# Attention with top-32 masking and a channel mix: twelve transposes of the identity for each of the first 20 tiles, and a new order

## Chip, cores and metric

The kernel runs on one core of a Trainium2 chip. The metric is the time of one execution on the device in microseconds; the median of several runs is compared. The engines are TensorE (PE), VectorE (DVE), ScalarE (ACT), GpSimd (POOL) and SyncE (SP, which here issues most DMAs). PEld is TensorE's loading of the stationary operand.

## The reference

For each of 8 batches and 8 heads, attention over 576 rows with head size 64, in which a row keeps only its 32 largest scores. The heads are joined to rows of 512, and a channel mix follows.

```python
scores = scale * np.matmul(q, k.transpose(0, 1, 3, 2))
kth = np.partition(scores, -top_k, axis=-1)[..., -top_k:-top_k + 1]      # top_k = 32
scores = np.where(scores >= kth, scores, -1000000000.0)
attn = np.exp(scores - np.max(scores, axis=-1, keepdims=True))
attn = attn / (np.sum(attn, axis=-1, keepdims=True) + 1e-09)
x = np.matmul(attn, v)                    # then (B, S, H * D)
...
xk = mu_k * x + (1.0 - mu_k) * x_prev     # x_prev: the row before
xr = mu_r * x + (1.0 - mu_r) * x_prev
k = np.maximum(xk @ w_k, 0.0)             # 512 to 1024
v = k * k @ w_v                           # 1024 to 512
r = 1.0 / (1.0 + np.exp(-(xr @ w_r)))
return r * v
```

## The kernel before

The attention is cut into 288 tiles of 128 rows by 576 columns, in 64 visits (batch, half of the rows, pair of heads). For one tile, TensorE computes the scores (`score` and `sliver`, L836 to L845, for two tiles at once), ScalarE copies them out of PSUM (`keep`, L850), VectorE finds the top values in seven pieces and then over all pieces (`cand`, `best`, `drop`, L855 to L860), GpSimd and ScalarE prepare the exact 32nd value (`under`, `count`, `below`, L866 to L871), VectorE picks it (`eighth`, `nine`, L872 and L874), ScalarE takes the exponential (`exps`, L877), and VectorE masks (`mask`, L880). TensorE then turns the masked tile in four transposes (`turn`, L885) plus one for the last 64 columns of two tiles (`turnl`, L894), ScalarE copies the result out (`et`, `el`), TensorE multiplies with v (`weigh`, L907 and L908), and VectorE scales the sum and puts it into `xT`, the input of the mix (`place`, L940 and L943).

The mix works on 18 chunks of 256 rows. GpSimd and ScalarE form the mixed input and split it in a high and a low part (`change`, `share`, `add`, `xh`, `xl`, L1009 to L1023), in two halves of the channels. TensorE multiplies each product three times, for the parts (L629 to L631): `hidden`, `gate` and `value`. The weights of the mix are unpacked at the start from pieces that DMAs bring (`weight`, L1085 to L1119), 20 blocks: eight of w_k, four of w_r (blocks 8 to 11), eight of w_v (blocks 12 to 19). In each, ScalarE, VectorE (`wshift` L1107, `wexp` L1112 or L1115, `wrest` L1117) and GpSimd (`wput` L1110 or L1114, `wmul` L1119) take part.

Three PSUM buffers called `rot` serve in turn the transposes, the mix's results and two steps of each weight block (`wabs` writes one that `wshift` reads, `wrest` one that `wfine` reads).

The order of work on each engine is written out ahead by a planner (`Plan.run`). Each step has a lane, a cost, its dependences and a key: the number of its tile plus an offset by name (`OFF`, with `FIRST`, `HEAD` and `TAIL` added at the beginning and the end). Among the steps of an engine that could start within `NEAR` of the earliest, the one with the lowest key goes first. Chunks are due by `AT` and `STEP`, the blocks of w_k, w_r and w_v by `WAT`, `LWAT`, `VWAT` and their steps, as in

```python
key = WAT + n * WSTEP if name == "k" else LWAT + n * LWSTEP if name == "r" else VWAT + n * VWSTEP
```

The engines then follow that order strictly; only the waits for data and buffers are left to the chip. The planner also has a model of TensorE's clock (`Clock`). One step called `warm` exists before: twelve transposes of the identity into a `rot` buffer at the very start (L1165), which nothing reads.

Of the kernel before, what the change touches and what calls it, by code (L numbers as in the profile page):

```python
# [37 lines left out]
OFF = dict(kt=-149.064, kq=-2.447, v=48.118, zero=104.971, score=-11.554, keep=-135.674, cand=6.552, best=-17.933, drop=-182.956, under=-102.12,  # L38
           count=-18.516, below=-102.498, eighth=9.321, nine=-50.972, exps=1.133, mask=-104.109, turn=-50.435, et=29.287, turnl=-30.586, el=-75.416,
           weigh=-30.634, inv=-20.812, inv2=-135.01, turni=-51.051, ri=36.948, place=-115.941, lowest=61.461, ranks=-134.855, mu=49.321, nmu=-39.508,  # L40
           changek=138.702, sharek=94.164, addk=371.12, xhk=24.993, xlk=-36.33, sharer=185.332, addr=48.759, xhr=89.136, xlr=-20.192, hidden=37.203,
           relu=-241.476, sq=56.91, r2=31.986, hl=54.569, gate=371.368, gexp=-213.982, value=170.367, gated=-58.13, store=-42.377, w=98.749,
           wabs=-68.48, wshift=-51.265, wsign=-219.747, wexp=100.695, wfine=-65.07, whi=-150.349, wmul=130.665, spread=-57.351, sliver=-131.257,
           low=-35.741, lowt=224.106, lowr=-284.336, lowc=45.392, wrest=-86.41, wm=235.872, wput=20.784, warm=99.586)
CANDS, BESTS = 0.117, -2.501
STEP, WAT, WSTEP, GATE, VALUE, PACE = 17.949, 2.161, 10.191, 3.223, 5.257, -2.0
# [20 lines left out]
BONUS = {("S", "W"): -33.418, ("T", "W"): 15.751, ("R", "W"): -30.909, ("T", "S"): 43.457, ("R", "S"): 49.885, ("W", "S"): -6.906, ("S", "R"): 36.783, ("T", "R"): 80.901, ("W", "R"): 94.651, ("R", "R"): 7.145, ("S", "S"): 77.39, ("R", "T"): 24.499, ("W", "W"): 40.464, ("Z", "S"): -129.751, ("W", "Z"): 71.854, ("S", "T"): -42.48, ("Z", "W"): -24.105, ("Z", "R"): 67.5, ("T", "Z"): 89.886, ("S", "Z"): -8.015, ("R", "Z"): 22.532, ("Z", "Z"): -71.918, ("Z", "T"): -14.968, ("W", "T"): 46.183, ("T", "T"): 3.444}  # L67
# [9 lines left out]
FIRST = dict(kt=9.824, kq=-62.943, v=-7.675, zero=98.267, score=-88.574, keep=25.077, cand=79.22, best=-29.451, drop=34.008, under=-44.481,  # L77
             count=-127.038, below=49.932, eighth=18.033, nine=10.948, exps=-14.36, mask=16.168, turn=-256.513, et=-60.13, turnl=-83.593, el=-13.794,
             weigh=-260.993, inv=-50.965, inv2=3.265, turni=-147.57, ri=147.35, place=-108.029, ranks=17.752, mu=-58.715, nmu=-156.45,
             changek=-29.419, sharek=-4.307, addk=-163.022, xhk=-50.628, xlk=-9.955, sharer=25.165, addr=164.205, xhr=170.896, xlr=133.774,  # L80
             hidden=96.642, relu=0.545, sq=-37.562, r2=115.817, hl=14.536, gate=-161.398, gexp=-55.717, value=-74.447, gated=159.726, store=210.93,
             w=56.679, wabs=-227.205, wshift=-93.047, wsign=-16.424, wexp=-30.394, wfine=-79.085, whi=-11.933, wmul=-42.277, spread=-24.769,
             sliver=51.45, wrest=39.226, wm=-303.52, wput=-24.756, low=83.408, lowr=-56.354, lowest=31.336, lowc=58.647, lowt=-61.014, warm=-7.404)
HEAD = dict(sharek=-70.074, zero=132.48, lowt=-39.544, store=225.857, el=-126.117, gate=-70.119, turni=111.107, sq=28.568, hl=61.165, relu=-14.297,
            wmul=-44.021, low=-21.718, xhk=28.236, inv=115.831, v=-51.162, gated=-129.248, xlk=-0.117, turn=40.157, r2=45.071, xlr=19.366,
            addr=-165.161, ri=-78.566, below=-8.543, best=-17.781, wabs=-86.745, lowr=134.423, sliver=-82.002, nmu=9.399, kq=160.097, changek=27.051,
            count=-9.443, hidden=66.556, addk=-87.675, xhr=104.686, lowc=84.506, eighth=-58.165, w=141.91, kt=-10.884, wshift=-13.321, wexp=-8.43,
            ranks=142.708, spread=48.261, mask=-39.589, whi=123.677, drop=-118.7, gexp=49.552, keep=-138.746, inv2=-12.512, mu=-108.325,
            weigh=-103.636, turnl=25.74, score=-76.981, under=-103.491, nine=-89.251, place=24.804, sharer=58.037, et=-8.177, wfine=-20.05,
            wsign=-173.139, exps=-57.171, lowest=-65.114, value=140.622, cand=-8.009, wrest=-4.191, wm=-7.658, wput=-29.71, warm=23.458)  # L90
TAIL = dict(addr=83.707, wshift=-99.353, wexp=96.445, sq=187.355, lowt=-151.412, sliver=-139.369, whi=-38.32, xlk=48.2, xhk=84.256, store=-74.037,
            nine=25.418, best=87.475, lowr=86.936, hl=97.628, turni=-78.124, xhr=72.803, relu=-35.414, kt=-29.128, drop=64.837, gate=-78.823,
            eighth=-59.927, under=25.811, inv2=-93.695, v=54.202, w=-106.308, wmul=-55.614, wfine=97.246, lowest=-122.151, gexp=120.926,
            score=-1.911, sharek=-46.119, wabs=-131.815, exps=22.349, nmu=-219.708, below=41.819, changek=-48.432, lowc=-8.068, inv=338.652,
            low=-35.808, gated=98.664, turnl=32.405, place=105.089, ri=117.337, r2=-73.571, weigh=-94.945, spread=-190.521, kq=-26.094, cand=63.03,
            value=42.206, hidden=-49.814, zero=106.116, ranks=-16.901, mu=134.337, count=48.088, mask=103.11, wsign=19.05, xlr=59.381, keep=-49.002,
            addk=60.223, el=-37.043, sharer=-138.117, turn=6.568, et=-21.007, wrest=62.833, wm=-176.605, wput=-87.431, warm=-32.933)
# [89 lines left out]
class Plan:  # L187
# [8 lines left out]
    def buf(self, name):  # L196
        return Buf(self.kinds[name])
# [226 lines left out]
def topk_attention_channel_mix(ctx: ExitStack, tc: tile.TileContext, q, k, v, mu_kr, w_k, w_v, w_r, out):  # L424
# [359 lines left out]
    def attend(plan, visits, X, pair_sums):  # L784
# [8 lines left out]
        for p, (b, hp, part) in enumerate(visits):  # L793
# [21 lines left out]
            for i in part:  # L815
# [48 lines left out]
                def sn(T, w):  # L864
# [415 lines left out]
```

## Time and profile before

| | |
|---|---|
| median of 3 runs | 1150.0 us (1149.75 to 1151.17) |
| profiled execution, its own time | 1152.01 us |
| its span, first to last instruction | 1150.2 us |
| mean granted TensorE clock | 0.978 |
| TensorE busy | 1088.8 us (95%) |
| VectorE busy | 1063.4 us (92%) |
| ScalarE busy | 1005.8 us (87%) |
| GpSimd busy | 930.0 us (81%) |

The shares are averages over a head, a long middle part and an end, which have to be read apart. The granted clock is a record of the throttle on TensorE: 1.00 is 2.4 GHz, and a stretch wholly at 1.2 GHz would show 0.50. In rows of instructions the first number is the start in microseconds from the beginning of the span, the second how long the merged group took, `x` how many instructions it holds; a bracket at the end gives the idle time of the engine before the group and what ended it.

### The profile page before, as it was taken

To read this page: it belongs to the slowest core of one execution; us is meant where nothing else is said; L and a number is where in the kernel's file an instruction comes from. 1 tells how busy PE (TensorE), PEld (TensorE's weight loads), DVE (VectorE), ACT (ScalarE), POOL (GpSimd) and SP (SyncE) were. 2 spreads that over 40 slices of the span, in tenths; PEclk is the share of its full clock that TensorE was granted. 3 is DMA by queue.
4 is the path that set the end of the run, shared out by engine and by line. 5 is a ranking of instruction groups with operands and counts; after the bars stand their busy time and mean duration, and the time that the engine had idled before them with its cause. 6 is when DMAs were issued, how large, how long until landed. Compare 5 with 4: busy or idle time off the path is not lost. (4 is left out here: it accounts for less than half of the span.)

```text
span 1150.2 us, 27623 instructions
## 1 busy us (share of the span) xinstructions
PE 1088.8 (95%) x8637; PEld 844.7 (73%) x8637; DVE 1063.4 (92%) x5741; ACT 1005.8 (87%) x2129; POOL 930.0 (81%) x1153
## 2 busy tenths in 40 slices
PE   6556789999999999999999999999999999999998
PEld 3343567778787777777777878787878787877886
DVE  7999999999999999999999999999999999999600
ACT  6878999999999999999999989999999989889641
POOL 4787898788887888878799888888797889788773
PEclk9777999999999999999999999999999999999999
DMA  8743332211221112111211112111221122110000
GB/s 281 265 133 105 126 105 79 70 55 34 77 72 42 53 60 84 57 65 56 76 59 43 58 58 79 50 56 65 67 68 34 44 82 78 51 39 22 20 19 22
DMA packets 38891, 83.64 MB, mean 73 GB/s; under 512 B 4432, under 2 KB 12624, under 8 KB 38736
## 3 DMA queue, kind: packets, MB, share of 16 engines
q1 hardware_dynamic: 38448, 81.41, 21.5%
q8 instruction: 70, 1.15, 0.4%
q14 instruction: 85, 0.70, 0.2%
q10 hardware_dynamic: 288, 0.39, 0.1%
HBM read 72.35 MB, written 9.44 MB: 71 GB/s over the span
## 5 line engine op out<-in xcount | busy, mean ns | idle before, releaser
L871 POOL TENSOR_TENSOR sg<-sc,sg 128x576 f32<-128x576 f32 x288 | 410.0, 1426 | 83.5 <-ACT sg L869 79.7
L855 DVE MAX8 cand<-sc 128x8 f32<-128x82 f32 (+1 forms) x2016 | 378.0, 230 | 4.8 <-ACT sc L850 3.8
L877 ACT ACTIVATE se<-sc,seen 128x576 f32<-128x576 f32 x288 | 216.4, 751 | 23.6 <-DVE E L880 21.7
L869 ACT ACTIVATE sg<-sc,seen 128x576 f32<-128x576 f32 x288 | 224.8, 781 | 12.8 <-POOL seen L866 11.6
L880 DVE SCALAR_TENSOR_TENSOR E<-sc,seen,se 128x576 f32<-128x576 f32 x288 | 230.9, 802 | 0.7 <-ACT se L877 0.5
L885 PE MATMUL rot<-ident,E 128*128 128x128 f32 x1152 | 183.3, 284 | 40.9 <-DVE E L880 37.4
L850 ACT ACTIVATE sc<-ps 128x576 f32<-128x576 f32 x288 | 186.6, 653 | 36.7 <-DVE E L880 18.0
L872 DVE MAX8 top<-sg 128x8 f32<-128x576 f32 x288 | 214.4, 745 | 3.2 <-POOL sg L871 3.1
L885 PEld LDWEIGHTS rot<-ident,E 128*128 128x128 f32 x1152 | 134.4, 144 | 97.5 <-DVE E L880 35.5
L857 DVE MAX8 top<-cand 128x8 f32<-128x56 f32 x864 | 176.4, 206 | 2.4
L887 ACT ACTIVATE et<-rot 128x512 f32<-128x512 f32 x288 | 172.3, 602 | 5.8 <-PE rot L885 5.0
L629 PE MATMUL rot<-xh,wk 128*128 128x256 f32 x576 | 169.8, 295 | 1.9 <-ACT et L887 1.5
L907 PE MATMUL ps<-et,v 128*64 128x128 f32 (+1 forms) x2560 | 159.7, 268 | 2.2 <-ACT el L896 2.0
L630 PE MATMUL rot<-xl,wk 128*128 128x256 f32 x576 | 161.3, 280 | 0.0
L631 PE MATMUL rot<-xh,wk 128*128 128x256 f32 x576 | 161.3, 280 | 0.0
L907 PEld LDWEIGHTS ps<-et,v 128*64 128x64 f32 x2560 | 132.7, 139 | 35.5 <-ACT el L896 17.1
L845 PE MATMUL ps<-K,qs 64*128 64x512 f32 x512 | 153.9, 680 | 0.0
L629 PEld LDWEIGHTS rot<-xh,wk 128*128 128x128 f32 x576 | 109.2, 190 | 18.7 <-issue 10.3
L629 PE MATMUL rot<-wv,hh 128*128 128x512 f32 x288 | 121.1, 420 | 0.0
L860 DVE MATCH_REPLACE8 cand<-top,cand 128x56 f32<-128x56 f32 x576 | 115.6, 201 | 0.2 <-issue 0.2
L631 PE MATMUL rot<-wv,hl 128*128 128x512 f32 x288 | 113.4, 394 | 0.0
L630 PE MATMUL rot<-wv,hh 128*128 128x512 f32 x288 | 112.5, 391 | 0.0
(88 smaller groups left out, 2234.2 us busy)
## 6 DMA issues: line engine op xcount, KB each, us to landing
K<-in_k SPq DMA_DIRECT2D x64, 320.0 KB, 2.9
v<-in_v SPq DMA_DIRECT2D x64, 320.0 KB, 2.9
out<-eb SPq DMA_DIRECT2D x35, 256.0 KB, 2.0
qs<-in_q SPq DMA_DIRECT2D x32, 160.0 KB, 2.9
stage<-in_moe_w_k SPq DMA_DIRECT2D x8, 512.0 KB, 5.4
xT<-in_moe_w_v SPq DMA_DIRECT2D x8, 512.0 KB, 4.2
stage<-in_moe_w_k SPq DMA_DIRECT2D x8, 511.5 KB, 5.1
xT<-in_moe_w_v SPq DMA_DIRECT2D x8, 511.5 KB, 3.5
```

The costliest lines, as they stand in the source:

```text
L629: return [nc.tensor.matmul(ps, lhsT=sh, rhs=mh, start=first, stop=False), nc.tensor.matmul(ps, lhsT=sh, rhs=ml, start=False, stop=False), ...
L630: nc.tensor.matmul(ps, lhsT=sh, rhs=ml, start=False, stop=False),
L631: nc.tensor.matmul(ps, lhsT=sl, rhs=mh, start=False, stop=last)]
L850: return nc.scalar.activation(T.sc.t, sl.t[:, o:o + S], AF.Copy)
L855: lambda T=T, c=c: nc.vector.max(T.cand.t[:, 8 * c:8 * c + 8], T.sc.t[:, CUTS[c]:CUTS[c + 1]]), reads=[T.sc], writes=[(T.cand, c)])
L869: lambda T=T, sn=sn: nc.scalar.activation(T.side.t, T.sc.t, AF.Sign, bias=sn(T, 1), scale=-BELOW, accum_out=T.top.t[:, TOPK:TOPK + 1]),
L871: plan.op(POOL, "below", n, 1375, 1430, lambda T=T: nc.gpsimd.tensor_mul(T.side.t, T.sc.t, T.side.t), reads=[T.sc], writes=[T.side])
L872: plan.op(DVE, "eighth", n, 660, 754, lambda T=T: nc.vector.max(T.top.t[:, 24:32], T.side.t), reads=[T.side], writes=[(T.top, 3)])
L877: plan.op(ACT, "exps", n, 667, 754, lambda T=T, pe=pe, sn=sn: nc.scalar.activation(pe.t, T.sc.t, AF.Exp, bias=sn(T, 0), scale=SCALE), read ...
L880: lambda T=T, U=U, pe=pe, sn=sn, i=i: nc.vector.scalar_tensor_tensor(T.e(), T.sc.t, sn(T, 2), pe.t, op0=OP.is_ge, op1=OP.mult, accum_out=U ...
L885: return [nc.tensor.transpose(pt.t[:, c * 128:(c + 1) * 128], E.t[:, o + c * 128:o + (c + 1) * 128], ident) for c in range(NKC)]
L907: return [*[nc.tensor.matmul(pa[hs[j]], lhsT=vs[j][:, c, :], rhs=es[j].et.t[:, c * 128 + o:c * 128 + o + m], start=(c == 0), stop=False) f ...
```

## The change

Each of the first 20 tiles (`n < FILLED`) gets two more steps named `warm` on TensorE (`FILL`), each with six transposes of the identity into a `rot` buffer that nothing reads. The planner may place them only after the mask of the tile. All numbers that the order is drawn from are new: the offsets, the due times and the limits.

```diff
+FILL, FILLED = 2, 20
...
-STEP, WAT, WSTEP, GATE, VALUE, PACE = 17.949, 2.161, 10.191, 3.223, 5.257, -2.0
+STEP, WAT, WSTEP, GATE, VALUE, PACE = 17.949, -2.953, 10.279, 3.785, 4.715, -2.0
...
-NEAR = dict(PE=191.859, ACT=75.568, DVE=1.085, POOL=435.734, SP=22.861)
+NEAR = dict(PE=200.511, ACT=80.856, DVE=1.034, POOL=365.747, SP=5.038)
...
-LWAT, LWSTEP = 32.287, -4.896
-VWAT, VWSTEP = -6.088, 6.336
-AT = [-8.312, -6.356, 61.244, 47.695, 89.808, 70.459, 99.171, 120.432, 150.299, 106.034, 145.652, 144.446, 197.402, 187.882, 242.002, 249.152, 147.142, 289.127]
+LWAT, LWSTEP = 46.576, -6.259
+VWAT, VWSTEP = -7.26, 5.224
+AT = [-3.746, -7.413, 59.993, 47.643, 93.32, 68.053, 86.932, 118.091, 138.824, 101.272, 146.526, 140.619, 178.873, 207.046, 228.967, 253.423, 146.649, 279.777]
...
-                plan.op(DVE, "mask", n, 728, 822,
+                masked = plan.op(DVE, "mask", n, 728, 822,
...
+                for _ in range(FILL if n < FILLED else 0):
+                    w = buf("rot")
+                    plan.op(PE_, "warm", n, 650, 850, lambda w=w: [nc.tensor.transpose(w.t[:, :128], ident, ident) for _ in range(6)], writes=[w], mode="T", after=[masked])
```

The tables `OFF`, `CANDS`, `BESTS`, `BONUS`, `FIRST`, `HEAD` and `TAIL` are replaced in the same way. In `OFF`, `turn` goes from -50.435 to -53.656 and `warm` from 99.586 to 90.408.

## Rows read from the trace of the kernel before

**Rows 1.** The page: busy tenths of two engines in 40 slices of 28.8 us

```profile
PE   6556789999999999999999999999999999999998
...
DVE  7999999999999999999999999999999999999600
```

**Rows 2.** Busy time by stretch: us, each engine (instructions), TensorE's clock, DMA share, GB/s

```profile
core 0: us, PE busy (x) PEld busy (x) DVE busy (x) ACT busy (x) POOL busy (x), PEclk, DMA share, GB/s
...
18.00:35.00 17.00, 11.63 (x44) 6.39 (x46) 16.92 (x66) 15.79 (x31) 13.56 (x14) 1.00 0.87 316
...
18.00:112.00 94.00, 55.00 (x313) 33.15 (x315) 92.86 (x405) 79.11 (x159) 73.09 (x78) 0.81 0.56 189
106.00:126.00 20.00, 13.09 (x87) 7.50 (x86) 19.79 (x97) 17.89 (x39) 17.19 (x20) 0.83 0.36 120
126.00:155.00 29.00, 24.83 (x200) 18.72 (x204) 28.91 (x154) 27.42 (x58) 25.79 (x30) 0.88 0.34 112
155.00:1090.00 935.00, 933.44 (x7696) 733.13 (x7689) 914.69 (x5055) 859.27 (x1837) 781.23 (x989) 1.00 0.18 59
1090.00:1145.00 55.00, 54.56 (x333) 48.47 (x331) 2.69 (x5) 18.67 (x33) 32.33 (x28) 1.00 0.06 21
```

**Rows 3.** Who waited for whom, 18 to 112 us: total us, times, longest

```profile
PE rot L885 <- DVE E L880: 34.2, 12, 5.5
...
DVE top L872 <- POOL sg L871: 1.0, 1, 1.0
```

**Rows 4.** Instructions in order of time around the start of the mix

```profile
105.78 0.42 DVE L943 TENSOR_TENSOR xT<-ps,ri 128x256 f32<-128x256 f32 x1
...
107.15 1.46 POOL L1110 TENSOR_TENSOR eb<-eb,r 128x512 f32<-128x512 f32 x1
...
109.67 1.04 POOL L1009 TENSOR_TENSOR xd<-xT 128x512 f32<-128x512 f32 x1
...
112.46 1.27 POOL L1119 TENSOR_TENSOR wv<-xT,r 128x512 fp32r<-128x512 f32 x1
...
112.73 0.91 ACT L1014 ACTIVATE xm<-xd,mu 128x256 f32<-128x256 f32 x2
...
115.16 1.10 POOL L1019 TENSOR_TENSOR xm<-xm,xT 128x512 f32<-128x512 f32 x1 [0.24 <-ACT xm L1014]
...
116.39 0.63 ACT L1021 ACTIVATE xh<-xm 128x512 fp32r<-128x512 f32 x1
...
122.83 2.51 POOL L1023 TENSOR_TENSOR xl<-xm,xh 128x512 fp32r<-128x512 f32 x2
...
125.94 0.39 PE L629 MATMUL rot<-xh,wk 128*128 128x256 f32 x1 [1.20 <-ACT et L887]
...
141.13 1.28 POOL L1110 TENSOR_TENSOR eb<-eb,r 128x512 f32<-128x512 f32 x1
```

**Rows 5.** TensorE's instructions in order of time: turns, one transpose, scores

```profile
18.51 1.11 PE L885 MATMUL rot<-ident,E 128*128 128x128 f32 x4 [3.12 <-DVE E L880]
...
96.52 2.08 PE L845 MATMUL ps<-K,qs 64*128 64x512 f32 x4
...
99.74 0.33 PE L894 MATMUL ps<-ident,E 128*128 128x128 f32 x1
...
108.04 1.13 PE L845 MATMUL ps<-K,qs 64*128 64x512 f32 x4
...
163.07 0.60 PE L885 MATMUL rot<-ident,E 128*128 128x128 f32 x4
```

**Rows 6.** TensorE's first instructions in order of time

```profile
1.42 2.82 PE L1165 MATMUL rot<-ident 128*128 128x128 f32 x12 [1.42 <-POOL ident masks.py:199]
```

**Rows 7.** VectorE's groups by line, 0 to 120 us: busy us, mean ns

```profile
L880 DVE SCALAR_TENSOR_TENSOR E<-sc,seen,se 128x576 f32<-128x576 f32 x21 | 16.8, 798 | 0.0
...
L1107 DVE TENSOR_SCALAR eb<-rot 128x512 uint32<-128x512 uint32 x16 | 10.8, 675 | 0.1
...
L1117 DVE TENSOR_SCALAR rot<-xT 128x512 uint32<-128x512 uint32 x8 | 5.4, 679 | 0.0
...
L1112 DVE TENSOR_SCALAR r<-eb 128x512 uint32<-128x512 uint32 x4 | 4.3, 1064 | 0.0
```

More of the change, by code (lines that the diff above doesn't have):

```diff
@@ L76 @@
+AT = [-3.746, -7.413, 59.993, 47.643, 93.32, 68.053, 86.932, 118.091, 138.824, 101.272, 146.526, 140.619, 178.873, 207.046, 228.967, 253.423, 146.649, 279.777]
 START = 24
[L77 to L97, printed above, removed]
+FILL, FILLED = 2, 20
@@ new lines @@
+FIRST = dict(kt=-17.505, kq=-72.232, v=-0.141, zero=62.549, score=-76.91, keep=11.317, cand=74.194, best=-41.853, drop=25.504, under=-39.342,
+             count=-128.085, below=67.752, eighth=7.562, nine=30.582, exps=-14.529, mask=31.309, turn=-287.274, et=-67.413, turnl=-80.546,
+             el=-21.343, weigh=-316.537, inv=-47.497, inv2=-10.838, turni=-151.544, ri=117.814, place=-101.884, ranks=-7.782, mu=-53.862,
+             nmu=-109.936, changek=-8.093, sharek=22.722, addk=-154.565, xhk=-49.377, xlk=-10.491, sharer=73.2, addr=193.472, xhr=143.196,
+             xlr=117.847, hidden=75.809, relu=-25.244, sq=-67.198, r2=136.421, hl=50.548, gate=-196.636, gexp=-34.007, value=-52.908, gated=148.293,
+             store=195.845, w=18.471, wabs=-215.128, wshift=-81.563, wsign=-22.615, wexp=-50.869, wfine=-113.755, whi=31.046, wmul=-39.321,
+             spread=-17.152, sliver=52.003, wrest=9.855, wm=-298.769, wput=-39.677, low=61.737, lowr=-85.399, lowest=7.817, lowc=78.635,
+             lowt=-47.354, warm=-24.036)
@@ new lines @@
+HEAD = dict(sharek=-76.499, zero=102.916, lowt=-54.186, store=226.567, el=-102.01, gate=-70.228, turni=125.077, sq=23.432, hl=77.491, relu=-12.022,
+            wmul=-32.666, low=-23.707, xhk=34.145, inv=116.744, v=-57.33, gated=-112.286, xlk=-11.889, turn=19.896, r2=48.776, xlr=34.256,
+            addr=-144.403, ri=-76.863, below=-0.406, best=-18.556, wabs=-78.354, lowr=138.891, sliver=-67.197, nmu=22.52, kq=147.53, changek=14.377,
+            count=-8.111, hidden=88.239, addk=-78.355, xhr=104.76, lowc=55.385, eighth=-70.565, w=139.891, kt=-14.743, wshift=-10.174, wexp=-2.601,
+            ranks=172.134, spread=47.064, mask=-40.944, whi=160.819, drop=-114.733, gexp=20.585, keep=-146.076, inv2=-32.327, mu=-119.097,
+            weigh=-108.856, turnl=19.972, score=-91.07, under=-77.986, nine=-83.629, place=28.23, sharer=38.632, et=-9.231, wfine=-45.636,
+            wsign=-208.01, exps=-49.707, lowest=-87.185, value=125.068, cand=6.403, wrest=4.53, wm=-31.071, wput=-34.257, warm=27.622)
@@ new lines @@
+TAIL = dict(addr=80.389, wshift=-110.2, wexp=65.909, sq=177.961, lowt=-122.144, sliver=-134.998, whi=-52.922, xlk=50.587, xhk=69.859, store=-108.679,
+            nine=32.747, best=96.467, lowr=84.665, hl=126.391, turni=-70.539, xhr=55.321, relu=-38.115, kt=-49.08, drop=59.74, gate=-81.511,
+            eighth=-69.021, under=18.809, inv2=-89.298, v=51.126, w=-110.154, wmul=-51.057, wfine=82.42, lowest=-123.584, gexp=148.548, score=-0.279,
+            sharek=-44.42, wabs=-117.072, exps=40.245, nmu=-239.115, below=46.324, changek=-53.292, lowc=-22.646, inv=333.629, low=-36.29,
+            gated=120.44, turnl=33.502, place=122.876, ri=132.788, r2=-88.318, weigh=-92.793, spread=-191.492, kq=-11.367, cand=82.551, value=47.187,
+            hidden=-52.882, zero=107.572, ranks=-6.635, mu=150.86, count=53.042, mask=100.311, wsign=18.962, xlr=68.124, keep=-44.303, addk=61.409,
+            el=-62.891, sharer=-138.556, turn=18.366, et=-38.453, wrest=33.162, wm=-182.427, wput=-83.573, warm=-32.072)
```

18 lines of the change are left out of this document (9 added, 9 removed).

## The prediction

> **What bounds the kernel now.** I read the page's slices first, then the busy time by stretch, then who waited for whom in the head, and last the instructions in order of time around the place where the bound changes hands. The slices show three stages [rows 1]: in slices 2 to 5 VectorE stands at 9 while TensorE stands at 5 to 7; after that both stand at 9; at the end VectorE is at 0 and TensorE works alone. By stretch [rows 2]: from 18 to 112 us VectorE is busy 92.86 of 94 us and TensorE 55.00; from 155 to 1090 TensorE is busy 933.44 of 935, and from 1090 to 1145 it is busy 54.56 of 55. So the head belongs to VectorE (top-k of the first tiles and the preparation of the weights), and from about 155 us TensorE never stops. From there on the time is the TensorE work that is left. What happens earlier counts only if it gets more useful TensorE work done before 155 us, or makes that work possible sooner.
>
> What keeps TensorE idle in the head is VectorE: 34.2 us of its waits between 18 and 112 us are transposes of a tile that wait for the mask, while VectorE itself waited once, 1.0 us, for GpSimd [rows 3]. The channel mix starts at 125.94, when the second half of chunk 0's input is ready [rows 4].
>
> **TensorE's clock in the head.** Its record gives 1.00 for 18 to 35 us [rows 2], but durations contradict it: the four transposes of a tile took 1.11 us at 18.51 and 0.60 at 163.07; a pair's score matmuls took 2.08 us at 96.52 and 1.13 at 108.04 [rows 5]. The head starts at the lower level (1.2 GHz) and later goes back and forth between it and 2.4 GHz: granted clock 0.81 from 18 to 112 us, the false part of the record included, 0.83 and 0.88 in the two stretches after it [rows 2]. The change aims at this.
>
> **The change, part by part.**
>
> 1. *Work added.* 20 tiles get two steps of six transposes of the identity: 40 steps, 240 transposes. No such step is in this stretch, so I bound it. At 2.4 GHz one transpose takes 0.33 and four take 0.60 [rows 5], so each further one is 0.09 and six are 0.33 + 5 x 0.09 = 0.78; 40 are 31 us. At 1.2 GHz the twelve at 1.42 us took 2.82 [rows 6], half of which is 1.41; 40 are 56 us. TensorE is idle 94 - 55.00 = 39.0 us between 18 and 112 [rows 2]. Twenty-one masks run in the first 120 us [rows 7], so the 20 tiles end near the end of that stretch. At the upper level the added work fits even without the time that the faster clock frees. I take that value, since part of the stretch is fast already: 0 us on the path. The other end is 56 - 39 = 17 us.
>
> 2. *Work made faster.* Seven pairs of scores between 18 and 112 us ran at about 2.08 and would save 0.95 each; twelve groups of transposes ran near 1.11 and would save 0.51 each; one of either and its fast counterpart stand in [rows 5]. That is 6.7 + 6.1 = 12.8 us of TensorE time. None of it lies on the path: VectorE, which sets the pace, waited 1.0 us in all, and not for TensorE [rows 3]. If the cover were gone, that is if VectorE were ahead of TensorE, the 12.8 us would count. Gain 0, at most 1.0.
>
> 3. *Waits added.* A filler needs one of the three `rot` PSUM buffers, so it may wait for whoever reads that buffer, ScalarE (`et`, `wfine`) or VectorE (`wshift`). Behind it on TensorE stand the next tile's turn and score, and who waits for those are ScalarE's `et` and `keep`, and then VectorE. The other way round, the next user of the buffer waits for the filler: ScalarE's `wabs` and VectorE's `wrest` (L1117, 16 in the first 120 us, in two groups of eight [rows 7]). If each of the 16 waited for one whole filler, 16 x 0.78 = 12.5 us would be added. I take 0, since there are three buffers and VectorE waited for none of them in this stretch [rows 3]; both ends stay. The filler steps have the key of their tile with a late offset (90.4 for `warm` against -53.7 for `turn`), so the planner puts them where nothing better is ready. They issue no DMA, and no queue but TensorE's gets an instruction.
>
> 4. *The new order.* Every offset, the chunks' due times and the weights' due times are drawn anew, so any step may be moved, with its loads on SP's queue. What this can win lies where TensorE lacks input after the first 16 tiles: 20 - 13.09 = 6.9 us from 106 to 126 and 29 - 24.83 = 4.2 us from 126 to 155 [rows 2], 11.1 us together. The first of these is a queue. From the place at 105.78 to the start of the mix at 125.94, half 1 of chunk 0 needs a change (1.04), two shares (0.91), an add (1.10), a split on ScalarE (0.63) and half of the pair at 122.83 on GpSimd (1.26): 4.9 us of work in 20.2 us [rows 4]. Ahead of it on GpSimd stand pieces of the value weights: 1.46 at 107.15 and 1.27 at 112.46, with another 1.28 at 141.13 in the second stretch [rows 4]. The new due times of these weights (`VWAT`, `VWSTEP`) lie 14 to 22 tiles earlier for blocks 12 to 19. If these three pieces are gone from here, the mix advances by 1.46 + 1.27 + 1.28 = 4.0 us. The ends are 11.1 us won, and the loss that the same weights bring if they go ahead of chunk 0 on VectorE (rival C). I take 4.0, between nothing and 11.1, because these are the pieces whose due times are seen to move. After 155 us I take 0: TensorE is idle there for 1.6 + 0.4 us [rows 2], so a new order can change only how often it switches between kinds of matmul. For that no row has a price; with the same pieces it can go either way by some us, which the range holds.
>
> The profiled execution took 1152.0 us for a span of 1150.2 and lies 2.0 over the median of 1150.0; the terms are differences and carry over. Sum: 1152.0 + 0 + 0 + 0 - 4.0 = 1148.0 on its own base, which is **1146.0** against the median.
>
> **A rule that speaks against it.** After the twelve transposes at 1.42 us [rows 6] the turn at 18.51 still took 1.11 us [rows 5], and no row shows a rise of the clock that transposes alone brought on. The Trainium skill ("TensorE: Matmul & The Clock Gate", Part 4: PE-mode transpose) says that in one kernel transposes did not bring on the full clock, as they do not count as busy the way matmuls do. By that rule the fillers would run at the lower level and lift nothing, which is rival D below. The head mixes transposes with scores and weighs, so this trace does not decide it.
>
> **Rivals.** A difference of 0.2% (2.3 us) is about what a measurement of this kernel can tell from no change.
>
> A, the forecast: fillers hidden, the mix starts earlier; 1139 (all 11.1 us won) to 1147.7, most likely 1146.0. Chance 0.45.
>
> B: fillers hidden, but the mix starts when it did, because VectorE still sets when tiles are done and the queue after the place keeps its length. Nothing that TensorE's clock does in the head reaches the end: 1150.0, within 2.3. VectorE's 92.86 of 94 us speaks for it [rows 2], the 15.3 us of queueing against. It is also the outcome if the change doesn't do what it says: fillers that do not lift the clock but fit. Chance 0.27.
>
> C, slower: the value weights go ahead of chunk 0 on VectorE. One block costs it 0.68 + 1.06 + 0.68 = 2.4 us (L1107, L1112, L1117) [rows 7]. Four of the eight had their L1112 in the first 120 us [rows 7]; three more ahead of the place at 105.78 put the mix off by 7.2 us, of which about 2 of the 4.2 us idle after 126 come back, since less stands in its way there: 1150 + 5 = 1155, with 1152.3 to 1158 around it. It decides from the first block on, as soon as the place moves by over 2.3 us. That VectorE has no slack speaks for it; that the queue after the place may shrink by as much, against. Chance 0.20.
>
> D, slower: the fillers run at 1.2 GHz and push TensorE behind. 56 us against 39 leave it 17 us late at 112 us; of the 11.1 us idle from 106 to 155 most come back, some 8, as the mix itself starts no later than its inputs: 1150 + 9 = 1159. It decides from the point where 40 steps cost more than 39 us, 0.98 each. The slow turns of [rows 5] speak for it, the fast half of the head against. Chance 0.08.
>
> **How the numbers follow.** The likeliest is A, 1146.0. The range runs from 1139, the end of A, to 1157; outside are D, the top of C, and what a change in the switching adds to A, together under 0.2. A alone is 1139 to 1147.7. Faster is A, 0.45; same is B, 0.27; slower is C and D, 0.28.
>
> **What would show it.** Step 1: two groups of six transposes a tile of about 0.78 us each; TensorE's busy time from 18 to 112 us up by 31 - 12.8 = 18 us, VectorE's still above 91 of 94. Step 2: turns near 0.6 and scores at 1.13 through the head. Step 3: no new wait of VectorE for `rot`. Step 4: the first hidden matmul some 4 us before 125.94, and the last matmul earlier by as much. I am wrong if the start of the mix moves and the end does not, if a filler takes 1.4 us, or if the stretch after 155 us changes its length by itself.

## The result, and the profile after

The changed kernel takes 1156.9 us (median of 3 runs, 1156.57 to 1157.85) against 1150.0: a ratio of 1.0059, 95% interval 1.0036 to 1.0082. The forecast was 1146.0, faster; the kernel came out slower, at the upper edge of the range. The profiled execution took 1157.85 us for a span of 1156.0. It lies 1.0 us above its median, that of before 2.0 above its own, so two traces laid side by side differ by 5.8 us where the medians differ by 6.9.

Line numbers of the changed kernel are those of before plus 2 up to the filler (L886) and plus 5 behind it: a turn is L890, `et` L892, `keep` L852, the mix L631 to L633.

The page of the changed kernel, busy tenths of two engines in 40 slices; compare [rows 1]:

```profile
PE   7687799999999999999999999999999999999997
...
DVE  7999999999999999999999999999999999999300
```

Its busy time by stretch: length, then busy us (instructions) of PE, PEld, DVE, ACT and POOL, granted clock, DMA share, GB/s; compare [rows 2]:

```profile
18.00:35.00 17.00, 12.48 (x63) 9.52 (x63) 16.76 (x67) 15.01 (x29) 13.76 (x14) 0.89 0.81 274
18.00:112.00 94.00, 71.92 (x530) 56.47 (x531) 93.52 (x411) 78.72 (x157) 72.92 (x79) 0.85 0.57 193
106.00:126.00 20.00, 18.27 (x163) 14.28 (x160) 20.00 (x102) 18.77 (x40) 16.30 (x20) 1.00 0.39 117
126.00:155.00 29.00, 23.37 (x202) 16.90 (x200) 28.18 (x150) 27.16 (x58) 27.91 (x34) 0.94 0.32 97
155.00:1090.00 935.00, 930.13 (x7654) 728.15 (x7655) 913.99 (x5052) 858.25 (x1839) 779.74 (x987) 1.00 0.19 59
300.00:800.00 500.00, 497.16 (x4085) 386.49 (x4083) 496.05 (x2772) 465.46 (x999) 419.69 (x533) 1.00 0.19 60
1090.00:1151.00 61.00, 59.10 (x353) 52.38 (x351) 3.44 (x5) 18.59 (x33) 33.08 (x29) 1.00 0.06 23
```

The kernel before has this for the 500 us in the middle:

```profile
300.00:800.00 500.00, 499.94 (x4128) 390.50 (x4129) 496.35 (x2768) 466.71 (x1001) 425.32 (x538) 1.00 0.19 60
```

Up to 155 us the change did roughly what it should: TensorE is fuller and its clock higher. From 155 us on it did not: TensorE is busy 930.13 of 935 us, where it was 933.44. Between 300 and 800 us it now waits (who waited for whom in the changed kernel, TensorE: total us, times, longest):

```profile
PE rot L631 <- ACT et L892: 1.7, 3, 1.0
PE ps L838 <- ACT sc L852: 0.4, 1, 0.4
PE rot L890 <- DVE E L882: 0.2, 1, 0.2
```

The kernel before has no such wait in this stretch. Where the time ends up is seen at the end: the last turn of a tile, the last matmul of the mix and the issue of the last store, in order of time. In the kernel before:

```profile
1084.41 0.60 PE L885 MATMUL rot<-ident,E 128*128 128x128 f32 x4
...
1144.18 0.39 PE L631 MATMUL rot<-wv,hl 128*128 128x512 f32 x1
...
1145.39 0.36 ACTq L1070 DMA_DIRECT2D out<-eb  x1
```

In the changed kernel:

```profile
1083.15 0.60 PE L890 MATMUL rot<-ident,E 128*128 128x128 f32 x4
...
1148.72 0.39 PE L633 MATMUL rot<-wv,hl 128*128 128x512 f32 x1
...
1149.93 0.36 ACTq L1075 DMA_DIRECT2D out<-eb  x1
```

Of the 5.8 us between the spans, 4.5 are there when the last matmul starts. The other 1.3 lie behind the last store's issue, from which it takes 4.8 us to the end of the span before and 6.1 after. In the other traces of one pass this takes 4.5 to 6.4 us, with the late part of the changed order 4.6 in one run and 6.4 in another; what sets it isn't shown. What follows is about the 4.5.

The last turn comes 1.3 us earlier than before, but 65.6 us of work stand behind it, where 59.8 stood. The groups of TensorE's instructions from the last turn on say which work the difference is. `value` in the kernel before:

```profile
L631 PE MATMUL rot<-wv,hl 128*128 128x512 f32 x37 | 14.4, 390 | 0.0
L629 PE MATMUL rot<-wv,hh 128*128 128x512 f32 x36 | 14.2, 395 | 0.0
L630 PE MATMUL rot<-wv,hh 128*128 128x512 f32 x36 | 14.0, 389 | 0.0
```

And in the changed kernel:

```profile
L633 PE MATMUL rot<-wv,hl 128*128 128x512 f32 x45 | 17.5, 390 | 0.0
L631 PE MATMUL rot<-wv,hh 128*128 128x512 f32 x44 | 17.3, 393 | 0.0
L632 PE MATMUL rot<-wv,hh 128*128 128x512 f32 x44 | 17.1, 390 | 0.0
```

These are 24 more matmuls of `value`, one every 0.23 us (the distance of their starts), so 5.5 us; all other groups have the same counts. The changed order had placed 5.5 us less of the mix ahead of the last turn. That turn should then have come 5.5 us earlier. It came 1.3 earlier, so TensorE lost 4.2 us on the way, and more if it had been ahead at first. The experiments ask where, and why.

### The profile page after: what moved, and what is told of

Its sections match the earlier page's. It is cut to its first block, busy times and chain, and to the rows that moved or that the text cites. A ratio compares the mean times of both kernels' runs of the same rounds, so it can differ in the third digit from the quotient of the medians.

```text
span 1156.0 us, 28120 instructions
## 1 busy us (share of the span) xinstructions
PE 1108.0 (96%) x8877; PEld 868.7 (75%) x8877; DVE 1063.1 (92%) x5741; ACT 1004.7 (87%) x2129; POOL 929.3 (80%) x1153
## 4 chain that ended last, share of the span: by engine, by line
PE 75%; DVE 16%; ACT 4%; POOL 3%; issue 1%; DMA 1%; SPq 0%; DVEq 0%; ACTq 0%
PE rot L631 13%; PE rot L633 13%; PE rot L632 12%; PE ps L912 10%; PE rot L890 9%; PE ps L847 9%; DVE cand L857 4%; DVE E L882 3%; DVE top L874 3%; PE ps L913 2%; PE ps L840 2%; DVE cand L862 2%; PE rot L935 1%; DVE top L859 1%; PE ps L845 1%; PE ps L899 1%
## 5 line engine op out<-in xcount | busy, mean ns | idle before, releaser
L852 ACT ACTIVATE sc<-ps 128x576 f32<-128x576 f32 x288 | 187.5, 655 | 37.1 <-DVE E L882 19.3
L890 PE MATMUL rot<-ident,E 128*128 128x128 f32 x1152 | 180.5, 282 | 25.9 <-DVE E L882 23.7
L890 PEld LDWEIGHTS rot<-ident,E 128*128 128x128 f32 x1152 | 132.3, 142 | 82.4 <-DVE E L882 29.2
L892 ACT ACTIVATE et<-rot 128x512 f32<-128x512 f32 x288 | 171.9, 602 | 5.0 <-PE rot L890 4.5
L631 PE MATMUL rot<-xh,wk 128*128 128x256 f32 x576 | 169.2, 294 | 1.0 <-ACT et L892 0.8
L633 PE MATMUL rot<-xh,wk 128*128 128x256 f32 x576 | 160.8, 279 | 0.0
L847 PE MATMUL ps<-K,qs 64*128 64x512 f32 x512 | 150.2, 664 | 3.3 <-ACT sc L852 3.0
L631 PEld LDWEIGHTS rot<-xh,wk 128*128 128x128 f32 x576 | 108.6, 188 | 18.5 <-issue 13.2
L631 PE MATMUL rot<-wv,hh 128*128 128x512 f32 x288 | 121.5, 422 | 0.0
L633 PE MATMUL rot<-wv,hl 128*128 128x512 f32 x288 | 113.3, 393 | 0.0
```

The source lines that it names most:

```text
L631: return [nc.tensor.matmul(ps, lhsT=sh, rhs=mh, start=first, stop=False), nc.tensor.matmul(ps, lhsT=sh, rhs=ml, start=False, stop=False), ...
L633: nc.tensor.matmul(ps, lhsT=sl, rhs=mh, start=False, stop=last)]
L847: return [nc.tensor.matmul(ps[h].t, lhsT=P.qs.t[w, c * 128:(c + 1) * 128], rhs=P.K.t[w, :MAIN], start=True, stop=True) for h, w in enumera ...
L890: return [nc.tensor.transpose(pt.t[:, c * 128:(c + 1) * 128], E.t[:, o + c * 128:o + (c + 1) * 128], ident) for c in range(NKC)]
```

## The experiments

One measure serves all of them. *Work done* at a moment is the number of matmuls and transposes of each kind up to there (from the grouped rows), without the fillers, times the time of one at the upper clock (the distance between starts); it is given as the lead over the kernel before, in us of TensorE. It is an estimate: another fair choice of these times moves a lead by some 0.5 us. The changed kernel leads by 2.1 at 155 us and by 2.3 at 300, then trails by 0.2 at 500, by 3.7 at 800 and by 4.4 at 1120. So 6.0 us go between 300 and 800.

Only part of that is idle time. TensorE's busy time in the stretch fell by 499.94 - 497.16 = 2.8 us; the other 3.2 lie in time in which it counts as busy, with its matmuls starting further apart.

The ratios compare each run with the kernel before run beside it, whose medians there were 1150.8 to 1151.8; a median of one experiment is therefore not to be set against 1150.0, or against that of another experiment, to the last microsecond.

Theory O: the late order loses the time, and the fillers are hidden. Rivals: F, the fillers cost it; H, the head leaves something behind that costs later.

### The fillers alone

The order of the change, with fillers that issue nothing:

```diff
-    plan.op(PE_, "warm", n, 650, 850, lambda w=w: [nc.tensor.transpose(w.t[:, :128], ident, ident) for _ in range(6)], ...
+    plan.op(PE_, "warm", n, 650, 850, lambda: [], ...
```

> The changed kernel with its order kept step for step, but the 40 filler steps emit no instruction. Theory O (the loss comes from the new order after about 300 us, where TensorE waits; the fillers are hidden): 1155 to 1160, nothing comes back, and turns of a tile in the head take 1.1 us again more often. Theory F (the fillers themselves cost the time, by holding TensorE or the rot buffers): about 1150, some 7 us come back.

Measured: 1159.6 us, ratio 1.0074 (1.0060 to 1.0088), as theory O expected. Between 300 and 800 us it loses 6.1 us, as with the fillers. F falls.

The order of before, with twelve transposes ahead of each of the first 20 turns:

```diff
+            if o.name == "turn" and 0 <= o.base < 20:
+                for _ in range(12):
+                    nc.tensor.transpose(o.bufs[1].t[:, :128], ident, ident)
```

> The kernel before with its order kept step for step, and twelve transposes of the identity put on TensorE right ahead of the turn of each of the first 20 tiles, into the buffer that this turn then overwrites. Theory O: within 0.2% of before, 1148 to 1152, with a higher granted clock in the head and VectorE as busy as before. Theory F: about 1157.

Measured: 1152.2 us, ratio 1.0004 (0.9995 to 1.0013). The granted clock from 18 to 112 us is 0.87, TensorE is busy 72.27 us there, and the time stays. In an order that wasn't planned for them, the fillers win nothing and cost nothing that can be told from none.

### Head of one order, rest of the other

Both orders are laid out; steps planned ahead of a cut follow the one, the others the other. The lines that set this (excerpt):

```diff
+HEADS, RESTS, CUT_AT = "after", "before", 155000.0     # e3; e4 the other way round
+HEADS, RESTS, CUT_AT = "after", "before", 186000.0     # e7
+HEADS, RESTS, CUT_AT = "before", "after", 190000.0     # e8
...
+    plan.forced = {o.n: (0, head[o.n]) if o.n in head else (1, rank.get(same.get(o.n), -1)) for o in plan.ops}
```

> Spliced order: each engine follows the changed kernel's order, fillers included, up to where it stood at about 155 us, and from there the order of the kernel before for all that is left. Theory O: the head's lead of about 2 us is kept and the later loss is gone, 1146 to 1149. Theory F, or a head that leaves something behind that costs later (theory H): 1155 to 1158.

> The opposite splice: the order of the kernel before up to about 155 us, without fillers, then the order of the changed kernel for all that is left. Theory O: 1157 to 1160, the loss of the late order without the head's lead. Theories F and H: 1149 to 1152.

Measured: 1158.7 (ratio 1.0068, 1.0054 to 1.0082) and 1164.1 (1.0106, 1.0091 to 1.0121). Both missed what was expected, and both stall at the seam: one wait holds TensorE there. (Lines of these kernels are 40 further than those of the changed kernel, so L880 is a score and L941 `el`.) In the first:

```profile
PE ps L880 <- ACT el L941: 6.8, 1, 6.8
```

In the second kernel:

```profile
PE ps L880 <- ACT sc L892: 4.2, 1, 4.2
```

Behind the seam they tell the orders apart all the same: with the rest of before the lag of 6.7 us at 200 us is 7.1 at 1120; with the rest of after, 7.9 at 200 grow to some 13 at 900. So the cut was put where both orders stand at the same steps.

> The splice of the third run with its seam some 30 us later (about 186 us), at a place where the steps that the two orders have done by then differ little. Theory O: without the 6.8 us wait that the first seam made, the head's lead of 1 to 2 us stays and nothing is lost later: 1147 to 1150. Theory H (the changed head leaves something behind that costs later): 1154 to 1158. The run shows which: if progress against the kernel before falls between 300 and 800 us, it is H.

> The opposite splice at about 190 us: the kernel before up to there, without fillers, then the order of the changed kernel. Theory O: progress level with before at 250 us, then a loss of some 6 us between 300 and 900 us: 1155 to 1159. Theory H: 1149 to 1152.

Measured: 1151.5 (ratio 1.0002, 0.9993 to 1.0011) with the head of the changed kernel and the rest of before, and 1156.6 (1.0045, 1.0031 to 1.0058) the other way round. The first keeps its TensorE busy from 300 to 800 us, as the kernel before does:

```profile
300.00:800.00 500.00, 499.51 (x4122) 390.16 (x4122) 495.72 (x2767) 465.98 (x1001) 424.40 (x537) 1.00 0.19 60
```

Its last matmul starts at 1144.17. The second loses 5.5 us from 250 to 800, and its last matmul starts at 1148.88; its time is as theory O expected. H falls: the loss comes with the late order, whatever the head. The time of the first missed the expected 1147 to 1150 all the same, because its lead was not kept: some 2.1 us at 155, 0.7 at 200 and nothing at the end. TensorE's waits from 155 to 200 us, of 0.9, 0.8, 0.4 and 0.4 us, amount to as much; the changed kernel has the first three too.

### The numbers planned anew

The tables of one kernel with the fillers of the other, so that the planner makes a third and a fourth order:

```diff
-FILL, FILLED = 2, 20
+FILL, FILLED = 0, 20          # e5, in the changed kernel; e6: the other way round
```

> The changed kernel's numbers, but planned without the filler steps, so the whole order comes out anew. Theory O with orders that scatter (any order from numbers not tried on it loses some us, at other places): 1152 to 1168, with the loss at other times than in the changed kernel. If the late loss hangs on the new numbers themselves and not on the one order: 1157 to 1161, with the same fall between 300 and 800 us.

> The numbers of the kernel before, planned with the filler steps. If orders scatter: 1152 to 1168. If only the new numbers are at fault: 1147 to 1151.

Measured: 1166.1 (ratio 1.0127, 1.0112 to 1.0143) and 1171.4 (1.0179, 1.0161 to 1.0197); the second is slower than either expectation. At 155 us they lead by 8.1 and 6.6 us; the first trails by 13.4 at 1090, the second by 17 at 1120. The first loses some 5.5 us between 300 and 800, about as the changed kernel does, and 10 more from 800 to 1090; the second has lost its lead and 7 us more by 200. Both leave 36 more matmuls of `value` behind the last turn than the kernel before, the changed kernel 24. A lead in the head says nothing of the end, and planning anew moves the time by more than the fillers do.

### Whose wait is it?

The largest wait of the changed kernel, in TensorE's instructions in order of time:

```profile
721.72 0.60 PE L890 MATMUL rot<-ident,E 128*128 128x128 f32 x4
723.28 0.51 PE L631 MATMUL rot<-wr,xh 128*128 128x512 f32 x1 [0.96 <-ACT et L892]
```

And what ScalarE does meanwhile:

```profile
721.41 0.76 ACT L879 ACTIVATE se<-sc,seen 128x576 f32<-128x576 f32 x1
722.09 0.65 ACT L852 ACTIVATE sc<-ps 128x576 f32<-128x576 f32 x1
722.62 1.09 ACT L892 ACTIVATE et<-rot 128x512 f32<-128x512 f32 x2
```

Two turns (719.69 and 721.72) and a small transpose (L935, 721.45) fill the three `rot` buffers, the mix's next block needs one, and ScalarE empties them only after an exponential and a copy of scores. Theory W takes such a wait for a local matter, which bringing the copy forward would end. Theory T says that ScalarE has no slack, so that the wait only moves.

```diff
+MOVES = [('ACT', 'et', 114, 1), ('ACT', 'keep', 131, 1), ('ACT', 'et', 132, 2), ('ACT', 'et', 187, 2)]   # engine, step, which, places earlier
...
+        seq.insert(at - back, seq.pop(at))
```

> The changed kernel with four steps of ScalarE moved and nothing else: the four copies (three et, one of them together with the keep ahead of it) that TensorE waits for at 461.66, 505.01, 528.24 and 722.62 us in the changed kernel's trace stand one or two places earlier in ScalarE's order, ahead of a count, a split, an el or an exps. The orders of the other four engines are untouched. Theory W (the waits that TensorE has between 300 and 800 us are part of the loss and are local: each comes from one step of ScalarE that stands in front of the copy): these four waits, 0.37 + 0.45 + 0.41 + 0.96 = 2.2 us, are gone, TensorE's busy time from 300 to 800 us rises from about 497.4 by some 2 us, the useful TensorE work done by 800 us rises from 3.7 us behind the kernel before to about 1.5 behind, and the time is 1154 to 1155, at least 1.5 us under the changed kernel's 1156.9. Rival T (ScalarE has no slack, so the stalls only move to the next copy or to a later step): waits of the same sum elsewhere, 1156 to 1158.

Measured: 1156.5, ratio 1.0047 (1.0034 to 1.0060). The four waits are gone, and others of about the same sum, 2.4 us, stand elsewhere, most of them now for VectorE and GpSimd. TensorE's waits from 300 to 800 us (lines of this kernel are 50 further than those of the changed kernel):

```profile
PE rot L985 <- POOL ri L981: 0.5, 2, 0.2
PE ps L890 <- ACT sc L902: 0.4, 1, 0.4
PE rot L985 <- DVE cand L907: 0.4, 1, 0.4
PE ps L890 <- DVE xT L998: 0.4, 1, 0.4
PE rot L940 <- DVE top L909: 0.3, 1, 0.3
PE rot L940 <- DVE E L932: 0.2, 1, 0.2
PE rot L940 <- ACT et L942: 0.2, 1, 0.2
```

The work lost from 300 to 800 us is 7.2 us. W falls and T holds, by the waits and the work lost; the time alone would not decide it, since the interval of its ratio overlaps that of the changed kernel. The same kind of edit in the kernel with the head of after:

```diff
+MOVES = [('ACT', 'et', 35, 2), ('ACT', 'el', 15, 2), ('PE', 'hidden', 6, 1)]
```

> The kernel whose order follows the changed kernel to about 186 us and the kernel before from there (1151.45 when it ran), with three steps moved to take the waits away that TensorE has between 155 and 186 us: one hidden group of the mix goes ahead of a turni on TensorE at about 155 us, and on ScalarE one et stands two places earlier and one el two places earlier. Theory O with W (the head of the changed kernel does win 2.1 us of TensorE work by 155 us, and the short waits between 155 and 186 us eat it): these waits (0.9, 0.8, 0.5, 0.4, 0.3 us, 2.9 together) shrink by half or more, the work done by 250 us stays 1 to 2 us ahead of the kernel before, and the time is 1148.5 to 1150.5. Rival (the lead is lost anyway, to other waits of the same sum, since the engines in front of TensorE have no slack there): 1151 to 1152, as without the moves.

Measured: 1151.1, ratio 0.9999 (0.9990 to 1.0008). In its trace the lead is 2.5 us at 300 and 1.4 at 1120. That is no gain of the moves: this execution led by some 1.2 us more than that without the moves at 155 us already, waits of 2.1 us from 155 to 250 are left of 3.0, and by 300 the lead has shrunk by 1 us or more. In the time there is no gain that can be told from none, as the rival expected.

### Relieving the engines that feed TensorE

From tile 70 on (about 300 us) steps read half their columns, which leaves part of the computation out; no order is touched. Theory S: VectorE, ScalarE and GpSimd have too little slack for this order. Rivals: V, VectorE alone sets the pace; L, TensorE's sequence costs by itself; G, GpSimd is the one.

```diff
-    lambda T=T: nc.vector.max(T.top.t[:, 24:32], T.side.t)
+    lambda T=T, w=S if n < 70 else S // 2: nc.vector.max(T.top.t[:, 24:32], T.side.t[:, :w])      # e11 to e15
-    lambda T=T, pe=pe, sn=sn: nc.scalar.activation(pe.t, T.sc.t, AF.Exp, ...)
+    lambda ..., w=S if n < 70 else S // 2: nc.scalar.activation(pe.t[:, :w], T.sc.t[:, :w], AF.Exp, ...)      # e13 to e16
...
+    # e13, e14: `count` and `below` on T.sc.t[:, :w] and T.side.t[:, :w] as well
```

> The changed kernel with VectorE relieved and no order touched: from tile 70 on (about 300 us) the maximum over the 576 corrected scores reads 288 of them, which leaves part of the computation out and takes about 0.3 us from each of 218 tiles, some 65 us of VectorE's 1063. Theory V (VectorE sets when each tile can be turned up to its last mask at about 1082 us, in both kernels; the changed order has 5.5 us less of the mix ahead of the last turn, so TensorE is short of work while VectorE paces it, and these 5.5 us stand behind the last turn, 65.6 us there against 59.8): without VectorE's pace TensorE goes through the same order with no such waits, its busy time from 300 to 800 us rises from 497.2 to about 499.5, the last turn comes some 5 us earlier, and the time is 1150 to 1152.5. Rival L (the changed order costs TensorE by itself: switches between kinds, copies on ScalarE, the three rot buffers): 1155 to 1157.5, as without the edit.

> The same edit in the kernel before, its order untouched: from tile 70 on the maximum over the corrected scores reads 288 of 576, which leaves part of the computation out. Theory V: here the order has 438.5 us of the mix ahead of the last turn, as much as TensorE gets done while VectorE works (busy 499.94 of 500 us from 300 to 800), so a faster VectorE wins little: 1148 to 1150.5, and the changed kernel with the same edit lies within 2.5 us of it. Rival L: 1148 to 1150.5 too, and the changed kernel with the edit 5 to 7 us above.

> The changed kernel with all three engines that feed TensorE relieved from tile 70 on (about 300 us), no order touched: the corrected scores are counted, multiplied and searched over 288 of 576 columns, and the exponential is taken of 288 of them, which leaves part of the computation out. That takes some 0.3 us per tile from VectorE, 0.7 from ScalarE and 0.7 from GpSimd, for 218 tiles. Theory S (TensorE loses because its order asks for tiles and copies sooner than the three engines, which have little slack, deliver them): the waits for et, sc and el between 300 and 800 us (3.2 us of them with VectorE alone relieved) go, TensorE is busy 499.5 us or more of these 500, the work lost from 300 to 800 against the kernel before with the same edit is under 1.5 us, and the time is 1148 to 1151. Rival L (the sequence on TensorE itself costs it: switches between kinds of matmul, the three rot buffers, a queue that holds it whatever the others do): the loss stays at 4 to 6 us, and the time at 1152.5 to 1155.

> The same edit in the kernel before, its order untouched: from tile 70 on counting, multiplying, searching and the exponential take 288 of 576 columns, which leaves part of the computation out. TensorE is full here already (500.00 of 500 us from 300 to 800 with VectorE alone relieved), so little is left to win: both theories expect 1147.5 to 1150. Theory S: the changed order with the same edit within 2 us of this one; rival L: 4 us or more above it.

> The changed kernel, order untouched, with VectorE and ScalarE relieved from tile 70 on: the maximum over the corrected scores and the exponential take 288 of 576 columns, which leaves part of the computation out. Theory S (the changed order leaves the feeding engines too little slack, and ScalarE's copies are what TensorE waits for): the work lost between 300 and 800 us, 4.7 us with VectorE alone relieved and 0.6 with all three, falls to under 2; TensorE busy 498.8 us or more of these 500; last matmul of the mix at about 1142, time 1149 to 1151.5. Rival G (GpSimd is the one that is short: its multiplication of 1.43 us per tile holds VectorE and with it TensorE): no change from VectorE alone, 1152.5 to 1154.5.

> The changed kernel, order untouched, with ScalarE alone relieved from tile 70 on: the exponential takes 288 of 576 columns, which leaves part of the computation out; VectorE keeps its 99% between 300 and 800 us. Theory S with ScalarE as the engine that is short: most of the gain of ScalarE and VectorE together, lost work from 300 to 800 under 3 us, time 1150.5 to 1153.5. Rival (VectorE and ScalarE are both short, and either alone frees little): loss 4 us or more, 1153.5 to 1156. Rival G: no change, 1156 to 1157.5.

| | median us | ratio (interval) | TensorE busy of 300 to 800 | work lost 300 to 800 | last matmul |
|---|---|---|---|---|---|
| after | 1156.9 | 1.0059 (1.0036, 1.0082) | 497.16 | 6.0 | 1148.72 |
| after, less ScalarE (e16) | 1154.1 | 1.0026 (1.0014, 1.0038) | 497.60 | 5.6 | 1146.16 |
| after, less VectorE (e11) | 1153.6 | 1.0022 (1.0013, 1.0031) | 497.19 | 4.7 | 1144.37 |
| after, less of both (e15) | 1149.7 | 0.9990 (0.9981, 0.9999) | 498.69 | 2.2 | 1142.06 |
| after, less of all three (e13) | (3769) | | 499.19 | 0.6 | 1141.27 |
| before | 1150.0 | 1 | 499.94 | 0 | 1144.18 |
| before, less VectorE (e12) | 1149.4 | 0.9991 (0.9981, 1.0000) | 500.00 | -1.1 | 1141.49 |
| before, less of all three (e14) | (3769) | | 500.00 | -1.5 | 1142.85 |

In the two runs with all three relieved, counting over half the columns made the kernel's own flag ask for its second pass, which works everything out again; their times are for both passes, and only the trace of the first pass is read.

In the stretch, ScalarE alone gives back 0.4 of the 6.0 us and VectorE alone 1.3; both together give back 3.8, all three 5.4. The waits go with them. TensorE's waits from 300 to 800 us with less VectorE:

```profile
PE rot L631 <- ACT et L892: 1.9, 3, 1.0
PE ps L838 <- ACT sc L852: 0.5, 1, 0.5
```

With less of VectorE and ScalarE:

```profile
PE rot L631 <- ACT et L892: 1.0, 2, 0.8
```

VectorE's relief alone left the waits for ScalarE and the 2.8 us of idle time as they were (busy 497.19); what it gives back lies in the time that counts as busy. So V falls, which expected some 499.5 us busy; its time, 1153.6, lies between what V and L expected. G falls as the only cause, since most of the gap closes with GpSimd at its full work. With all three relieved the changed order still does 2.1 us less in this stretch than the order of before (0.6 lost against 1.5 won). Of these, 0.8 are idle time, 0.7 of it one wait for a copy of ScalarE, so at most 1.3 are left for L. Even so its last matmul is then the earlier of the two, 1141.27 against 1142.85, since its head leads by 3.6 us at 300. S holds for the larger part. The last matmuls of e11, e15 and e16 read too well by 2.0 us: their profiled executions lead by 4.3 us at 300 us, ahead of the edit, where that of the changed kernel leads by 2.3. The column of the stretch is free of that. The times of e11 and e16 may gain from such a lead too; by their ratios either engine alone gives back more than in the stretch, some 4 of the 6.8 us, with 2.6 us either way on the changed kernel's ratio alone. The times of e15 and e16 are as theory S and as the rival of two short engines expected; in the stretch, e15 and e13 come a little short of what S expected (2.2 us lost for under 2, and 2.1 between e13 and e14 for under 1.5).

## Why the prediction was wrong

**The step that failed** is in part 4: "After 155 us I take 0: TensorE is idle there for 1.6 + 0.4 us [rows 2], so a new order can change only how often it switches between kinds of matmul." The 6 us went there, and not by switching: from 300 to 810 us TensorE changes its kind of work some 500 times in both (499 and 505, with turns, scores, weighing and the three products of the mix as kinds), and priced pair by pair of neighbouring kinds, by the distances of the kernel before, the new sequence from 300 to 800 us would be 0.5 us cheaper (an estimate). What [rows 2] showed, TensorE busy 933.44 of 935 us, was read as a property of the kernel ("From there on the time is the TensorE work that is left"). It was one of the order. The same row has VectorE at 914.69 and ScalarE at 859.27, and VectorE's last mask starts at 1082.87. Up to 1083 us VectorE is busy 912.68 of 928, 98.3%, in the kernel before:

```profile
155.00:1083.00 928.00, 926.44 (x7626) 727.33 (x7618) 912.68 (x5048) 854.13 (x1825) 774.96 (x982) 1.00 0.18 59
```

A turn mostly starts 1 to 4 us after its mask does, in both kernels. The order of before put just so much of the mix between the tiles that TensorE stayed full at the pace at which masks and copies come. The new order puts 24 matmuls less there, so TensorE waits (2.1 of the 2.3 us of waits that show are for ScalarE's copies), and the 24 stand behind the last turn, where no more tiles run beside them. That the 3.2 us within the busy time are waits of the same kind, too short to show, isn't read from rows; it is argued from the runs that relieved the feeding engines, in which they went as well. The longest entry of 0.6 us among TensorE's waits from 155 to 1090 us in the kernel before is evidence that its order fits, not that any order would.

The sum can be closed on the traces. The forecast was 4.0 us won. The changed kernel had done 2.1 us more by 155 us, did 6.5 less from there to 1120, and lost 1.3 behind the last store: 5.7 of the 5.8 us by which the spans differ.

**Part 1, work added, was right.** Six fillers take 0.82 us warm (predicted 0.78) and half of 2.77 us cold (predicted 1.41). TensorE's busy time from 18 to 112 us rose by 16.9 us (18), and VectorE stands at 93.52 of 94. Rival D didn't come, and the fillers do lift the clock: from 18 to 112 us the granted clock is 0.85 with them and 0.73 in the same order without. TensorE's instructions in order of time, in the changed kernel:

```profile
19.15 1.12 PE L890 MATMUL rot<-ident,E 128*128 128x128 f32 x4 [3.69 <-DVE E L882]
20.06 2.77 PE L886 MATMUL rot<-ident 128*128 128x128 f32 x12
22.62 1.06 PE L890 MATMUL rot<-ident,E 128*128 128x128 f32 x4
23.47 1.23 PE L886 MATMUL rot<-ident 128*128 128x128 f32 x6
24.63 1.13 PE L847 MATMUL ps<-K,qs 64*128 64x512 f32 x4
...
26.12 0.82 PE L886 MATMUL rot<-ident 128*128 128x128 f32 x6
```

In the same order without fillers:

```profile
19.22 1.12 PE L890 MATMUL rot<-ident,E 128*128 128x128 f32 x4 [3.69 <-DVE E L882]
22.57 1.11 PE L890 MATMUL rot<-ident,E 128*128 128x128 f32 x4 [2.23 <-DVE E L882]
23.94 2.08 PE L847 MATMUL ps<-K,qs 64*128 64x512 f32 x4 [0.26 <-ACT sc L852]
```

From 19.15 to 24.63 us TensorE did nothing but transposes, at the price of 1.2 GHz at first; the scores that follow took 1.13 us, the price of 2.4 GHz. Without the fillers they took 2.08. So transposes alone brought on the upper level here. The sentence of the Trainium skill ("TensorE: Matmul & The Clock Gate", Part 4: PE-mode transpose) that the full clock doesn't engage for them is not borne out in this kernel.

**Part 2, work made faster, was too small for this order.** Its gain was put at 0, at most 1.0. Without the fillers VectorE is busy 91.92 us from 18 to 112 us instead of 93.52 (one trace each), and `place` waits 2.7 us up to 126 for ScalarE and TensorE (1.2 for `ri`, 0.8 for `el`, 0.7 for the weighing). With them VectorE waits 0.2 us in all. The 1.0 was read from waits of an order that had no fillers.

**Part 3, waits added, was right:** no wait of VectorE for a filler shows; its one wait from 18 to 126 us is 0.2 us for ScalarE.

**Part 4 up to 155 us was right in its mechanism and too large.** The queue in the changed kernel, in order of time; compare [rows 4]. On VectorE:

```profile
107.02 0.41 DVE L948 TENSOR_TENSOR xT<-ps,ri 128x256 f32<-128x256 f32 x1
```

On GpSimd:

```profile
108.94 1.30 POOL L1115 TENSOR_TENSOR eb<-eb,r 128x512 f32<-128x512 f32 x1
...
111.55 1.06 POOL L1014 TENSOR_TENSOR xd<-xT 128x512 f32<-128x512 f32 x1
...
117.76 1.28 POOL L1024 TENSOR_TENSOR xm<-xm,xT 128x512 f32<-128x512 f32 x1
...
120.62 1.27 POOL L1028 TENSOR_TENSOR xl<-xm,xh 128x512 fp32r<-128x512 f32 x1
```

On TensorE:

```profile
123.42 0.38 PE L631 MATMUL rot<-xh,wk 128*128 128x256 f32 x1
```

From the place to the mix it takes 16.4 us, 3.8 less than before (predicted 4.0), with one piece of weights between instead of two. That the two numbers agree is in good part chance. The third piece of the sum, at 141.13, stands behind the start of the mix and could not delay it, so the two ahead made 2.7; and the one piece that went is worth 1.3 to 1.5 of the 3.8. The place comes 1.2 us later, so the mix starts 2.5 us earlier. Over all traces with this head and its fillers the start lies between 120.0 and 123.7 us (nine, mean 122.2), with the head of before between 124.5 and 126.5 (five, mean 125.3): 3.1 us. Without fillers the changed order starts at 126.47, with fillers the order of before at 128.06 (one trace each). So fillers and order seem to win this together, not the due times of the weights alone.

**Of the rivals** none was the one. C priced a loss of 7.2 us at the place, which came 1.2 us later, and the mix started earlier all the same; its time of 1155 was near by chance. B was what becomes of the change if the rest of the order is kept: 1151.5. A was right up to 155 us in direction, not in size, and assumed that a lead there reaches the end. The range held the time only just, and by luck: the loss after 155 us had been given "some us" and no row.

**What would show it** named the case: the start of the mix moves and the end does not, and the stretch after 155 us changes its length by itself.

**What stays open:** which of the new numbers moved the two blocks of `value` behind the last turn; what the rest of the 2.1 us is that the changed order loses even when it is well fed; what the 1.3 us behind the last store are; whether the fillers win any time in the end (1.0074 without them and 1.0059 with them, in intervals that overlap); and why fillers in the order of before start the mix later, at 128.06. No version was found that beats the kernel before.

## What to carry to other kernels

Where two or three engines are nearly full at once, a full engine in the trace shows that the present order fits, and a new order is to be priced from the slack of the engines that feed it, not from that engine's own idle time. Compare what each order leaves for the end, where the engine works alone: here a count of the matmuls behind the last turn, 24 more of 0.23 us, told of 5.5 us before any wait was read. A lead won early counts only if the order behind it has room to keep it: leads of 6.6 and 8.1 us at 155 us ended some 20 and 15 us slower.

## What was not expected of the hardware

Transposes alone, 18 of 26 of them of the identity, took TensorE from the price of 1.2 GHz to that of 2.4 GHz: scores 2.08 us without them and 1.13 behind them. And a kernel with the same order in its head starts its mix at times that differ by up to 3.7 us between executions (119.99 to 123.65), so that a difference of 2 us between two traces of a head is not yet one between two kernels.
